# A neural codec's residual: diagonal products on sixteen 32x32 places of TensorE instead of four 64x64 places

## The chip, the core and the metric

One core of a Trainium2 chip runs the whole program. The time is device time in microseconds (us), the median of three runs; the profile is of one further execution. TensorE (PE in the profile, its weight loads PEld) multiplies into PSUM; VectorE (DVE), ScalarE (ACT) and GpSimd (POOL) do elementwise work; SyncE (SP) issues the transfers.

## What is computed

The reference, cut to what matters. B = 2 sequences of T = 16000 tokens with D = 512 channels; four codebooks of 8 rows each.

```python
def reference(x, dw_enc, codebooks, dw_dec):
    z = silu(depthwise_conv3(x, dw_enc))          # B, T, D
    res, q = z, zeros_like(z)
    for s in range(4):                            # four stages of a residual quantizer
        cb = codebooks[s]                         # 8, D
        d2 = sum(res*res) - 2*res @ cb.T + sum(cb*cb)
        sel = cb[d2.argmin(-1)]
        q, res = q + sel, res - sel
    return depthwise_conv3(q, dw_dec)             # bfloat16
```

All of it is bfloat16, so each `res - sel` is rounded to bfloat16, and the last choice depends on those roundings.

## The kernel before

**Tiles.** The 32000 tokens are cut into 18 tiles of G x 128 tokens, G = 8, 10, 12, then twelve of 16, then 12, 10, 8 (`SIZES`, L202). Channels lie on the partitions, in KT = 4 blocks of 128; each tile lives in slots of the large array `XR`/`XT`, 128 tokens to a group g, and z overwrites x there.

**Stages of a tile.** `load` (L625) brings x by transposing transfers on SP's queue. `front` and `front2` (L661, L694) make z: the three taps, two sums, exponential, reciprocal and gate, on ACT and DVE. `products` and `gram` (L722, L704) compute norms and scores of one group against the codebooks on TensorE, as 128x32 weights and 64 columns. `select` (L734) decides stages 0 to 2 from the scores of z and the codebooks' own products; it leaves one-hot choices in `OHALL`, and GpSimd lays them out anew in `OHDS` (L790, L802). `resid` (L889) makes the residual before the last stage, again on TensorE, and writes it over z; then `products` once more and the last choice (`decide3`), `windows` (L862: the transposed one-hots) and `back` (L977: two products per 128 tokens, a copy out of PSUM into `YB`, and a store).

**The residual** (`resid`). It runs over the four channel blocks; call one pass of `unit(i)` a unit. There are 18 x 4 = 72. The groups g of the tile are dealt to four row groups r = g mod 4, because the one-hots of group g stand on partitions 32r to 32r+31; each r has a PSUM bank of its own, with a tile's G/4 groups of 128 columns (512 columns at G = 16; 384 and 256 at G = 10; 256 at G = 8). Into each bank go, one after another:

- z times the identity (`IDENT`), z times 2^16 (`UP`), later z times -2^16 (`DOWN`): the diagonal products (L910 to L914). Adding and taking away the lifted z makes PSUM round as the reference does.
- four `picks` (L916 to L919): the chosen codebook rows, weights `WR[v]` with 32 rows x 128 channels, four row groups at once.

Before, a diagonal product takes 64 channels to 64 partitions. For even r the two halves stay where they are, for odd r they swap (`half[r % 2 ^ ...]`, L913); so two values of r and two halves make four products on four 64x64 places of the array. IDENT, UP and DOWN take 8 such products each per unit, 24 in all, each with its own weight load.

A unit is two steps: `first` (IDENT and UP for r = 0, 1, into the first pair of banks) and `second` (IDENT and UP for r = 2, 3, picks 0 to 2, DOWN for all, the last picks). Then ACT or DVE copies each pair of banks back into `XR` (L941). Since odd groups have their channels swapped in halves, everything that is multiplied with them has to be swapped alike: the copies of the codebook for the last scores (`CBM2` and the last 2 x 32 columns of `XR`, L434 to L444, read in `gram` at L717) and the weights `WR` (made by `SEL3` and `spread`, L505 to L528).

**Order.** `Plan` (L17) holds every step with its engine, an assumed cost and what it depends on. The order on each engine is not worked out at run time: `RANK` is a written-out list with one rank for each step, which sorts the five engines' queues (PE, ACT, DVE, POOL, SP), and `WHERE` has a letter for each of the 610 steps that may run on ACT or DVE (copies out of PSUM, taps, the +1). `order` walks the queues with the assumed costs, hands out PSUM banks and, where it foresees TensorE standing idle, puts in filling products (`fill`, L1060) that keep its clock up. Assumed costs of the residual are at L932 to L935.

Of the kernel before, what the change touches and what calls it, by code (L numbers as in the profile page):

```python
# [8 lines left out]
BF16 = mybir.dt.bfloat16  # L9
# [176 lines left out]
def kernel(  # L186
# [8 lines left out]
    nc = tc.nc  # L195
# [14 lines left out]
    HB = 32  # L210
    ZW = HB + NC
    ROWX = SLOTS * P + 2 * NC
# [10 lines left out]
    RANK = ("000002000403000a02020c030d010b01010k020c0a0d07060g0t0a070d0b0e050e03050Q0S0R0T0d170r1b0f0i0a0D0J0X0m0b01070j0p0v0E0G0V0c"  # L223
            "0h0w0C0H0L0M0U06050i090g0q0e0c0o0f0f0k08080b090l0m04030x070j0w0y0A0C0E0G0I0m0p0t090v06080k0n0N0O0P0B0K110l0o0G0W13140g0y"
            "0M0105060e0n0o0t0u0x0y0A0h0A0i0w000f0L080k040V0z0s0C241T0F0q0I090s2a0r2b0B270w200i0g0j040m0n0l0r0h0K0q0p0o0h0u0x0s0z0l0O"
            "0r0S0u0W0n0p131615181a1c1e100q1i0t1j1r1p1s1u1w1y1A120z0N0A1C1I1O1Q1S1U1W150C0S0D0F0U0W0G0H11100I0L13190N0R1a180V112Q2V31"
            "36381b1r1f1w1v1J1S1g1v1C1M1L0v0D0F0H0s0P0J0U0y1f0M0N0B0j0Q0T0R0X0B1h06070d030k050h0b0a09040i080214121710190z1b1d0E1m0F1t"
            "0H1v0I290u0x1E0v1G1V1J1X222326160E0V0J2d2f2g2i2j2l2n2p190O140Q2r2u2t2w2z2B2D1c0S170T0U1c1h0W101g1f13151k1l1c1d1p1u1k1m3B"
            "1o3F3H3K3O3Q1w1H1B1K1I1P1P1E1L1G1R1K2c5b260D1g1k111n1l1o1q0L210u0r0q0n0j0l0o0w0p0v0x0e0c0f0m0g0t0s1z1x0K1B1M1D1H1N0Q251L"
            "1K0J1F0O0P1P1R0R280T2c0X2I152H0K0M2s0P2v2y2A2C2F2G2J1a0X1e122N2P2M2O2R2T2U2W1d161j193033323537393o1f1e1t1h1i3u1x1j1l3z1A"  # L230
            "1q1r1C3I1s1t1D1E1u1x3U1z404c4e4o4r1S2022282a2e2c242d2z2x2p1X29262b2d141734181a3e3i3h3n3r3t3v1e1n1z1p3y3E3D3G3J3L3N3S1g1y"
            "1G1A3V3X414446484b1h1K1Q1L1M1T1V1N1O1U1X1R1T22211U1V2725272b4X25285557595e5n2l2o2u2s2y2w2u2B2y2E2A2w2K2G2R2K2z2x2v2O2J2D"
            "0z0J0G0M0H0E0A0y0L0K0N0D0C0P0O0F0B0I2m2h2o2e2E122q2L1i3x2x162k1b1d2K2S2X1m3C0Q1714120T0S0V1118100X130U0W1916150R3d3b3c3a"
            "3f1n3g3j1s3w1q3l1o3k3m3q3p3s1y3A1B3M1F3W1I471N4t1D1J4h1F1H4k4m4n4q4s4v454y1i1W24214D4G4I4K4M4O4Q4T1j292c2d4V535456585a5d"
            "1n2e5i2f2h2k2j2j2k2m2l2m2o2p2q2p2s2t2u2D2F632A2J676h6m6p6r302P312S352U3b342T322W2M37313r3e343a6J3e332T1P1Q4z20234S52505c"
            "5f5h4i5j1k2g2h2i5p5s5m5r5v5x5z5B1o2r5F2t5E5I5J5L5O5R5T1p2C2z2G2H2D2E2M2N2I2H2Q2T2N2M2W2X2R2Q36386F3b3c6P6R6T737c3n393M3u"
            "3Q3A3q3v3g3z3j3d3D3m3N3w3l3y3l443I3D1b1n1p1d1h1l1e1k1f1i1g1j1c1r1q1m1o1a3P3R423T4f1O494j1S514g4d4a434l4p4u4x265g1H1s1G1w"
            "1F1A1C1E1u1y1x1I1B1v1z1J1D1t1W4w4A4B4H234E4P2a5k4J4L4C4F4R4N4U4W2f5o2g5l2i5q2r612B682n2q5G2v2w5N5P5Q5S5W605w621q2I2C2L65"
            "6e6a6k6n6q6v6A1s332V396C6I6H6K6O6Q6S1t3d6X3g3i35363j3k373a3l3p3b3c3q3w3h3i3B3C7H3F3I7J7M7Q7U843V3z4d8C4a3M3G3X3D4b3K3x42"
            "3F433H3y4w424y453T2P2S6u2U2V6y6L6G6N6U6W701u3f323h747972777d7f7i7k1v3s3d3u7m7o7r7t7v7x7A1w3A3k3E3G3o3p3H3J3r3s3K3L3x3t3T"  # L240
            "3U3B3C41468n48498p8s8u8x8J4n3V4x434E48404t414B463W4z444L4h424S4i4T4k441V211U221M1X2a251T1R1O1Q24281W231N1l1m5u5y5D5t5M5A"
            "5H662F6E5K5V2n5C5U645X692L6M292e2j2k2h2o2f2m2b2q2r2i272l2n2g181r2s6b6d6g6c6l6i6j6o2O6V6s6w6t6f6x6z6B6D2X7h3071347b387l3f"
            "7I3m3o7j3t3x7w7z7y7C7E7L7O1x3O3v3S7T828186888a8c8g1y453G478i8k8l8o8q8t8w1C4c8A4e4g3N3O4i4j3Q3T4k4l3U3R4p4s403X4A4D9m4K4M"
            "9w9B9D9F9L4X9Q554r5b4v4i514n564q4m544p574s4j594t5t4F4r3P3R8b3W408d8m8r8v8y8B8D1z4f8G4h8F8H8K8M8O8R8T8V1A4m3S4o9194929698"
            "9b9e1B4C474F4G4b4a4H4I4d4c4O4P4g4f4V504m4o585daa5c5fadagaiakaq5o4C5s4G5v4K4x5y4I5E4M4F5w4H5B4N4L5F4O5J4R4D202J2H2L2x2F2G"
            "2E2N2K2C2t2v2I2y2O2B2A78757a767p7u7e7B3n877n7g7s7q7D7F7G7K3y8I2Q37322X2R352V382S2P2U3936333a312W307N7V7P3q7R807X853E8z89"
            "837S7W8e8f8h8j3J8E3L8L3P8W3W9p499u4q4r934u4v979d999f9h9l9n1D4J9s4N9q9t9v9A9C9E9H9K1E4U4j4W9N9P9T9Va0a2a41G5aa75e5g4y4x5h"
            "5ianao5j5k4Aar5l5m4D4B5q5raD5u5zaLaOaTb8bc5V52615569594U62566f5e506b5b6e5d4T6457665a4W4Q4R9I5253a1abacaeahajal1F5nav5pap"
            "auaxazaBaCaEaG1H5x4J5CaIaKaNaQaSaUaW1I5G4P5K5L4S4T5M5N4V4W5R5T4X505W5X53546568bG6a6cbRbWc5c7c96pce6s5n6D5t576C5v6G5y5a6x"
            "5q6E5u566r5m6w5r533j3z3v3o3f3w3i3h3c3m3u3g3s3p3e3n3r3k8N8S8Q8P8U8X90954eaf9c9i9a9g9j9k9o9r4la93R3N3B3O3S3P3A3J3C3M3Q3F3K"  # L250
            "3t3H3L3I3E9M9J9G9y9Ua39Oa54uas9S9R9z9x9X9Wa6a84wam4zaw4EaJ4LaX4Qb55A5DaV5H5Ib1b4b3b7b9bbbd1K5Qbf5Sbibkbhblbnbpbtbv1L63bx"
            "67bBbFbEbIbKbMbO1M6d5c6g6h5h5g6i6jc3c46k6lca5j6n6q5lck6u6vcq6z6AcCcEcMcPcR6Ud4725L735M597q627v665c7adA7i5U5b705J775O585O"
            "5Pbg5U60bubAbzbHbQbTbX1S6mc66oc8cccbcdcfcgchcj1U6t5o6ycmcpcrcsctcvcx226B5s6I6J5x5z6M6N5B5C6O6P5E5D6Q6W5H5I7576dw7c7ddDdJ"
            "dNdTdW1Q1V7tej7M6e7W6j5e7N6f7R6g5f7T6i7V6k5g7D697Fex5d484f3V3U4g4h3X46414c4a494d4745434e4bataAaFayb0aHaMb24Uc2b6aRaPbabm"
            "bebjbr58c14l4k4w4p4A4z4t4s4B4n4y4q4u4obobqbsbybwbJbDbS5fczbLbNbC51bUbVbPc05icB5kcl5pcy5wcI5AcW6F6HcH6K6LcJcLcKcOcQcScV1X"
            "6S5F6Vd0d2d3d5d7d9dbdc2171df74dgdjdidldodqdr2878dz7e7f5Q5R7g7h5S5T7k7m61607r7s64ef7w7Aew7E7JeKeNeOeReW1R2086fd8d6s8g6t5i"
            "8c6r8ffh5h8i6u8lfx5k8a6q8m6v5j6R6Td86Xdedmdndpdtdud6dv2479dx7bdydKdCdHdMdPdSdU257n5X7pe0e2e4e5e8ecee277ueh7x7yepes7C7GeA"
            "eC7H7K6d6c7Q7SeU6h838bff8hfjfkfofrft1P1W8ofv8v6y8z6A5m8q6w8rfy5l8A6B8C6C5n4P4K4R4v4I4X4N4S4M4Q4C4OcicocwcncUcucAcX5GdhcN"
            "cFcGcDcTdad1dd5KdB5NdF5PdL7j7ldV7oe3e7ebedegeidkek297z677Bemeneqereteveyez2a7IeB7LeGeHeFeIeLeQeT2b7UeX7X80f86l81856n6m87"
            "886pfe8j8kfufs8p8wfA8sfBfCfDfEfF1T238BfH8F6E8I6G5o8M6H8LfQ5q8N6I5p4E52554H51544V4J4G1J1OdEdGdIdsdRdXdOe165eoe65VdQ5W63ea"  # L260
            "e9el68eu6aeD6beE7O7PeJePeMeSeVf1f0f22c82f384f5f6f4f7f9fafbfc2d896o8efgfiflfmfnfpfq2e8nfw8t8u6xfz8x8yfG6z8D8E6DfI8G8HfJ6F"
            "8J8KfKfLfMfNfO1N268OfP8P6J8Q6K5r8R6L8S6M5s")
    WHERE = ("DADDDAAAADAAAADDDDDADDDDDDDDDDDAAAAAAAAAAAAAAADDDDADDDDDADDDDDDDDADAAAAAAAAAAAAAAAADADDDDDDDDADDDDDDADAADAAADADAADAAAAAA"
             "AAAAAAAAAAAAAAAAAAAAAAADDDDDADDADAADDDDDDDADADADDDDAADAAAAAAAAAAAAAAADAADAAAAAAAAAAAAAAAAAADDDDDADDDDDDDDADDDDADDDDDDDDA"
             "ADAAAAAAAAADAAAAAAAAAAAAAAAAAAAAAAAAAAADDDDDDDDDADDDDDDDDDDDDDDDDDDAADAAAAAAAADAAAAAAAADAAAAAAAAAAAAAAAAAAADDDDDDDDDDDDD"
             "DDDDADDDDDDDDDDDADAADDADAAAAAAAAAAADAAAAAAAAAADAAAAAAAADDDDDDDDDDDDDDDDDDDDDDDDDDDDDDAAADDDAADDAAAADAAADAAAAAAAAAADAAAAA"
             "AADDDDDDDDDDDDDDDDDDDDDDDDDADDDADDAAAAAAADDAAADADAADADDDDDAADADAAADAADDDDDDDDDDDDDDADDDAAAADDDDAAADADDDDDDDDADAADDDADADD"
             "AADDADAAAA")
# [42 lines left out]
    CBM2 = sb([P, 2 * KT, NC], BF16, "CBM2")  # L311
# [37 lines left out]
    HF = P // 2  # L349
    PICK = 1.25  # L350
    WR = [sb([P, D], BF16, f"WR{v}") for v in range(4)]
# [51 lines left out]

    def setup():
# [22 lines left out]
        for i in range(KT):  # L427
            bx = {}
            ptb = lambda bx=bx: ps(bx).bitcast(BF16)[:, 0:NC]
            j = add("PE", 0.2, key, lambda i=i, p=ptb: nc.tensor.transpose(p(), CB1[:, i * P:(i + 1) * P], IDENT[0:NC, 0:NC]),  # L430
                    ["CB1", "I"], [], take=("S", bx), mm=1)
            j2 = add("ACT", 0.25, key, lambda i=i, p=ptb: nc.scalar.copy(CBT[:, i, :], p()), [], [("CBT", i)], after=[j])
            add("ACT", 0.25, key, lambda i=i, p=ptb: nc.scalar.mul(CBM2[:, i, :], p(), -2.0), [], [("CBM2", i)], free=bx, after=[j2])
        for i in range(KT):  # L434
            bx = {}
            ptb = lambda bx=bx: ps(bx).bitcast(BF16)[:, 0:NC]

            def turned(i=i, p=ptb):
                for h in range(2):
# [660 lines left out]
```

## Time and profile before

| | |
|---|---|
| median of 3 runs (lowest, highest) | 584.66 us (579.47, 587.69) |
| the profiled execution | 584.51 us |
| its span, first to last instruction | 582.2 us |
| mean granted TensorE clock | 0.951 of full |
| TensorE products, and weight loads | 12463 each |
| of these diagonal products (L914) | 1728 |
| of these filling (L1062) | 224 |

A row of a group in the profile gives line, engine, operation, what is written and read with the shape, and the count; then the time in which at least one of them ran, the mean length of one in ns, and the engine's idle time just before them with what ended it. A product's length includes its way through the array, so several in a row overlap; what a step costs TensorE is read from start to start. `64*64 64x512` is a product with 64x64 weights and 64 rows of 512 columns. A row of waits gives who waited for whom, the total in us, how often, and the longest. A row of a stretch gives its bounds and length, then each engine's busy time with its count of instructions, the granted clock, the share of the transfer engines and GB/s.

### The profile page before, as it was taken

How to read it: one execution, taken by the hardware profiler on the slowest of the kernel's cores; microseconds unless marked ns; L12 is line 12 of the kernel's file. 1: busy time of each engine (PE TensorE's matmuls, PEld its weight loads, DVE VectorE, ACT ScalarE, POOL GpSimd, SP SyncE). 2: the span in 40 equal slices, each digit the busy share in tenths (PEclk: the TensorE clock that was granted, in tenths of full speed). 3: DMA queues.
4: the chain of work that ended last, by engine and by line, in shares of the span. 5: the costliest groups of instructions: out<-in, count | busy, mean ns of one | idle time of the engine just before them, and what ended most of it. 6: DMA issues, size and time to landing. Idle time of an engine off the chain costs nothing.

```text
span 582.2 us, 27464 instructions
## 1 busy us (share of the span) xinstructions
PE 473.8 (81%) x12463; PEld 226.6 (39%) x12463; DVE 538.6 (93%) x1021; ACT 534.2 (92%) x430; POOL 109.0 (19%) x140
## 2 busy tenths in 40 slices
PE   6475878878787798877987798888898798989995
PEld 4232334424434244333434253334343354444442
DVE  5999999999999899999999999998999899988552
ACT  3889999989999999999999999998999989988554
POOL 6232102202002303050303024211204102010000
PEclk9688779979999899899999999898999999999999
DMA  7444546544455466756667665857886640311455
GB/s 248 99 92 100 89 95 94 85 91 75 85 159 118 83 129 120 187 127 119 124 153 131 150 143 109 196 91 163 145 139 129 183 130 3 112 75 40 159 190 174
DMA packets 153384, 71.81 MB, mean 123 GB/s; under 512 B 144710, under 2 KB 144742, under 8 KB 153012
## 3 DMA queue, kind: packets, MB, share of 16 engines
q1 hardware_dynamic: 153052, 69.64, 54.4%
q8 instruction: 97, 1.59, 1.2%
q10 hardware_dynamic: 216, 0.43, 0.2%
q14 instruction: 19, 0.16, 0.1%
HBM read 2.79 MB, written 32.77 MB: 61 GB/s over the span
## 4 chain that ended last, share of the span: by engine, by line
DVE 28%; ACT 25%; SPq 17%; PE 17%; issue 8%; DMA 4%; POOL 0%; ACTq 0%; DVEq 0%; POOLq 0%
SPq L631 13%; DVE XR L402 8%; ACT EX L700 6%; ACT XR L941 6%; ACT EX L689 4%; ACT YB L1006 4%; PE banks L914 4%; PE banks L997 4%; DVE EX L402 3%; PE banks L719 3%; SPq L1034 3%; DVE EX L682 3%; DVE TA L682 3%; PE banks L919 3%; DMA XR<-in_x_dram 2%
## 5 line engine op out<-in xcount | busy, mean ns | idle before, releaser
L402 DVE TENSOR_TENSOR XR<-XR,EX 128x4096 bf16<-128x4096 bf16 (+3 forms) x72 | 145.8, 2029 | 0.9 <-ACT EX L700 0.5
L1006 ACT CAST YB<-banks 128x1024 bf16<-128x1024 f32 x117 | 116.3, 1055 | 10.7 <-PE banks L997 5.1
L802 POOL COPY OHDS<-OHALL 128x256 bf16<-128x256 bf16 (+3 forms) x36 | 63.8, 1774 | 318.1 <-DVE OHALL L402 314.8
L689 ACT ACTIVATE EX<-XR 128x4096 bf16<-128x4096 bf16 (+3 forms) x36 | 115.9, 3218 | 2.2 <-DVE XR L402 2.0
L941 ACT CAST XR<-banks 128x1024 bf16<-128x1024 f32 (+2 forms) x120 | 106.7, 952 | 10.5 <-PE banks L919 10.5
L700 ACT ACTIVATE EX<-EX 128x4096 bf16<-128x4096 bf16 (+3 forms) x36 | 115.5, 3214 | 0.5 <-DVE EX L691 0.3
L719 PE MATMUL banks<-XR 128*32 128x64 bf16 x8064 | 92.6, 199 | 14.1 <-DVE XR L402 7.1
L719 PEld LDWEIGHTS <-XR 128*32 128x32 bf16 x8064 | 77.6, 97 | 60.4 <-issue 47.6
L919 PE MATMUL banks<-OHR,WR 32*128 32x512 bf16 (+2 forms) x1152 | 81.9, 357 | 0.0
L402 DVE TENSOR_TENSOR EX<-TA,EX 128x4096 bf16<-128x4096 bf16 (+3 forms) x36 | 72.7, 2020 | 0.0
L914 PE MATMUL banks<-XR,IDENT 64*64 64x512 bf16 (+2 forms) x576 | 57.8, 377 | 17.0 <-ACT YB L1006 3.4
L997 PE MATMUL banks<-WDEC,OHW 128*128 128x512 bf16 x190 | 58.7, 393 | 15.0 <-ACT YB L1006 4.7
L1062 PE MATMUL banks<-MSK,IDENT 128*128 128x512 bf16 x224 | 66.2, 437 | 4.9 <-DVE MSK L413 3.8
L914 PE MATMUL banks<-XR,UP 64*64 64x512 bf16 (+2 forms) x576 | 55.4, 363 | 0.0
L682 DVE TENSOR_SCALAR TA<-XR,WENC 128x2048 bf16<-128x2048 bf16 (+3 forms) x67 | 45.5, 683 | 5.1 <-DMA XR<-in_x_dram 3.1
L919 PEld LDWEIGHTS <-WR 32*128 32x128 bf16 x1152 | 23.6, 92 | 58.8 <-issue 52.9
L682 DVE TENSOR_SCALAR EX<-XR,WENC 128x2048 bf16<-128x2048 bf16 (+3 forms) x62 | 41.6, 683 | 1.0 <-DMA out_dram<-YB 0.9
L682 DVE TENSOR_SCALAR XR<-XR,WENC 128x2048 bf16<-128x2048 bf16 (+3 forms) x62 | 41.9, 685 | 0.0
L914 PE MATMUL banks<-XR,DOWN 64*64 64x512 bf16 (+2 forms) x576 | 41.4, 363 | 0.0
L691 DVE TENSOR_SCALAR EX<-EX 128x4096 bf16<-128x4096 bf16 (+3 forms) x36 | 39.5, 1101 | 0.0
L914 PEld LDWEIGHTS <-IDENT 64*64 64x64 bf16 x576 | 21.2, 105 | 44.8 <-issue 37.1
L1062 PEld LDWEIGHTS <-IDENT 128*128 128x128 bf16 x224 | 22.3, 109 | 32.1 <-issue 16.3
(137 smaller groups left out, 600.0 us busy)
## 6 DMA issues: line engine op xcount, KB each, us to landing
out_dram<-YB SPq DMA_DIRECT2D x34, 448.0 KB
out_dram<-YB SPq DMA_DIRECT2D x28, 512.0 KB
XR<-in_x_dram SPq DMA_TRANSPOSE x263
out_dram<-YB SPq DMA_DIRECT2D x28, 60.0 KB
XR<-in_x_dram SPq DMA_DIRECT2D x1, 1280.0 KB
XR<-in_x_dram SPq DMA_DIRECT2D x1, 1024.0 KB
out_dram<-YB SPq DMA_DIRECT2D x30, 2.0 KB
out_dram<-YB SPq DMA_DIRECT2D x2, 224.0 KB
```

Source lines behind the costliest of these rows:

```text
L402: add("DVE", cost, key, lambda: nc.vector.tensor_tensor(out=out, in0=a, in1=b, op=op), reads, writes, **kw)
L631: nc.sync.dma_start_transpose(out=X[:, :, g + 1, :], in_=src[g])
L682: lambda dst=to, src=src, w=w: nc.vector.tensor_scalar(out=dst, in0=src, scalar1=w, scalar2=None, op0=ALU.mult),
L689: add("ACT", act(nb * R), ("exp", n, i0), lambda: nc.scalar.activation(v(ex), Z, ACT.Exp, scale=-1.0), zt, ext + ["ACTTAB"], hold="E")
L700: nc.scalar.add_instruction(mybir.InstActivation(name=nc.get_next_instruction_name(), engine=mybir.EngineType.Activation, func=ACT.Reciprocal,
L719: nc.tensor.matmul(o[HB * q:HB * (q + 1), u * ZW:(u + 1) * ZW].rearrange("p (s c) -> p s c", s=2), lhsT=blk, rhs=both, start=False, stop=( ...
L914: nc.tensor.matmul(at(r)[to], lhsT=dia[h, h], rhs=Z[h, i, r:G:RG, :], start=start, stop=False)
L919: nc.tensor.matmul(at(r), lhsT=WR[v][g, i * P:(i + 1) * P], rhs=W[g, v // 3, 0:rows_of[r], :], start=False, stop=stop)
L941: either({"ACT": act_psum(2 * k * P), "DVE": dve(2 * k * P)}, key(1), lambda dst=dst, src=src: nc.scalar.copy(dst, src()), lambda dst=dst, ...
L997: nc.tensor.matmul(o, lhsT=W[:, k, PADC:PADC + P], rhs=WDEC[u], start=True, stop=not wrap)
L1006: either({"ACT": act_psum(1024), "DVE": dve(1024)}, key, lambda dst=dst, box=box: nc.scalar.copy(dst, ps(box)), lambda dst=dst, box=box: n ...
L1062: nc.tensor.matmul(PS[j // 2][:, 512 * (j % 2):512 * (j % 2) + NMK * ZW], lhsT=IDENT, rhs=MSK.rearrange("p u w -> p (u w)"), start=True, s ...
```

## The change

- The diagonal products become 32x32 blocks. Channels are rotated by r: quarter q of the block goes to quarter (q + r) mod 4 of the partitions, in the bank of r. Four quarters and four r are sixteen places. IDENT, UP and DOWN take 16 products each per unit, 48 in all.
- `first` now holds IDENT for r = 0, 1 alone (8 products); `second` has IDENT for r = 2, 3, UP for all four, the picks, DOWN and the last picks (56). The columns of a product and the picks are as before.
- What is multiplied with the residual is rotated alike: four copies of the codebook at the end of `XR` rather than two, written there straight from PSUM (`CBM2` and a copy by ACT go); twelve small transposes for each channel block rather than two; `SEL3` with four parts rather than two, and `spread` with seven products rather than three.
- Assumed costs follow (`DIAG`), and `RANK` and `WHERE` are new lists. One step fewer (the removed copy) is in `RANK`. In `WHERE` 306 letters are ACT's and 304 DVE's, where 315 and 295 were; of the `back` copies 112 and 14, where 117 and 9 were.

```diff
-    ROWX = SLOTS * P + 2 * NC
+    ROWX = SLOTS * P + 4 * NC
...
-    HF = P // 2
     PICK = 1.25
+    DIAG = 1.25
...
+    def turn_of(q, r):
+        at = HB * ((q + r) % RG)
+        return slice(at, at + HB)
...
             def turned(i=i, p=ptb):
-                for h in range(2):
-                    nc.tensor.transpose(p()[HF * h:HF * h + HF], CB1[:, i * P + HF * (1 - h):i * P + HF * (2 - h)], IDENT[0:NC, 0:NC])
+                for r in range(1, RG):
+                    for q in range(RG):
+                        to = turn_of(q, r)
+                        nc.tensor.transpose(p()[to, (r - 1) * NC:r * NC], CB1[:, i * P + HB * q:i * P + HB * (q + 1)], IDENT[0:NC, 0:NC])
...
-        add("ACT", 0.35, ("setup", 0.9, 0), lambda: nc.scalar.copy(XR[:, :, SLOTS * P:].rearrange("p i (h c) -> p i h c", c=NC),
-            CBM2.rearrange("p (h i) c -> p i h c", i=KT)), [("CBM2", i) for i in range(2 * KT)], ["ZC"])
...
-                    cb = SLOTS * P + (last and g % 2) * NC
+                    cb = SLOTS * P + (last and g % RG) * NC
...
-            def diagonal(dia, rs, start=False):
-                for r in rs:
-                    for h in half:
-                        to = half[r % 2 ^ (h is half[1])]
-                        nc.tensor.matmul(at(r)[to], lhsT=dia[h, h], rhs=Z[h, i, r:G:RG, :], start=start, stop=False)
+            def diagonal(dia, rs=range(RG), start=False):
+                for q in range(RG):
+                    for r in rs:
+                        h = turn_of(q, 0)
+                        nc.tensor.matmul(at(r)[turn_of(q, r)], lhsT=dia[h, h], rhs=Z[h, i, r:G:RG, :], start=start, stop=False)
...
             def first():
                 diagonal(IDENT, (0, 1), start=True)
-                diagonal(UP, (0, 1))
-
-            def second():
+
+            def products_of():
                 diagonal(IDENT, (2, 3), start=True)
-                diagonal(UP, (2, 3))
+                diagonal(UP)
                 for v in range(3):
                     picks(v)
-                diagonal(DOWN, range(RG))
+                diagonal(DOWN)
                 picks(3, stop=True)
-            c0, c1 = (mm(rows_of[2 * b] * P) for b in range(2))
+            c0 = mm(rows_of[0] * P)
...
-            j = add("PE", 2 * c0 + 0.09, key(0), first, ..., mm=8)
-            j = add("PE", 3 * c1 + c0 + RG * PICK * c0 + 0.28, key(1), second, ..., mm=32)
+            j = add("PE", DIAG * 0.5 * c0 + 0.09, key(0), first, ..., mm=8)
+            j = add("PE", DIAG * 2.5 * c0 + RG * PICK * c0 + 0.28, key(1), products_of, ..., mm=56)
```

129 lines of the change are left out of this document (65 added, 64 removed).

## Prediction

> **What bounds the kernel now.** I read the page first (engines, then the chain that ended last), then the busy time by stage, then the waits, then TensorE's instructions in order of time.
>
> ```profile
> span 582.2 us, 27464 instructions
> PE 473.8 (81%) x12463; PEld 226.6 (39%) x12463; DVE 538.6 (93%) x1021; ACT 534.2 (92%) x430; POOL 109.0 (19%) x140
> DVE 28%; ACT 25%; SPq 17%; PE 17%; issue 8%; DMA 4%; POOL 0%; ACTq 0%; DVEq 0%; POOLq 0%
> ```
>
> VectorE and ScalarE are busy 93% and 92% of the span, and the chain runs through them three times as long as through TensorE (53% against 17%). An average hides stages, so the next table cuts the span where the work changes:
>
> ```profile
> 40.00:440.00 400.00, 326.79 (x8773) 154.45 (x8772) 393.29 (x690) 391.96 (x288) 75.35 (x50) 0.95 0.61 122
> 440.00:519.70 79.70, 67.93 (x1950) 32.31 (x1949) 74.33 (x168) 76.77 (x63) 12.83 (x21) 0.98 0.39 105
> 519.70:531.30 11.60, 11.56 (x326) 5.42 (x326) 11.50 (x23) 9.36 (x9) 1.48 (x2) 1.00 0.27 94
> 531.30:571.90 40.60, 39.78 (x1127) 19.81 (x1125) 24.62 (x78) 24.97 (x31) 1.09 (x4) 1.00 0.41 141
> ```
>
> Columns after the length: PE, weight loads, DVE, ACT, POOL busy. From 40 to 440 us DVE idles 6.7 us of 400 and ACT 8.0: these two set the pace and TensorE has room. From 519.7 to 571.9 it is the reverse: TensorE is busy 51.3 of 52.2 us, and after 531.3, when the last front is done, DVE and ACT work 25 of 40.6 us each. This tail is TensorE's. The stage 440 to 519.7 lies between: DVE idles 5.4, ACT 2.9.
>
> How much do the element engines wait for TensorE before the tail (40 to 519.7 us)? These are the largest such rows, and two further rows that matter below:
>
> ```profile
> ACT XR L941 <- PE banks L919: 2.5, 3, 1.4
> ACT YB L1006 <- PE banks L1001: 1.5, 1, 1.5
> DVE RC L770 <- PE banks L823: 1.3, 1, 1.3
> ACT OT L816 <- PE banks L811: 1.2, 2, 0.9
> ACT YB L1006 <- PE banks L997: 1.1, 2, 0.7
> DVE TA L682 <- DMA XR<-in_x_dram: 3.1, 2, 2.4
> PE banks L719 <- issue: 6.1, 9, 1.0
> ```
>
> The first five add up to 7.6 us over two engines, so 3.8 us of time at most.
>
> **The change part by part.** *The diagonal products.* Two units of 512 columns, one whose halves stand together and one split by other work:
>
> ```profile
> 291.04 0.41 PE L914 MATMUL banks<-XR,IDENT 64*64 64x512 bf16 x4
> 291.59 0.70 PE L719 MATMUL banks<-XR 128*32 128x64 bf16 x64
> 292.23 0.60 PE L1062 MATMUL banks<-MSK,IDENT 128*128 128x512 bf16 x2
> 294.20 0.41 PE L914 MATMUL banks<-XR,IDENT 64*64 64x512 bf16 x4 [1.37 <-DVE PR L957]
> 296.40 0.41 PE L914 MATMUL banks<-XR,IDENT 64*64 64x512 bf16 x4
> 296.64 0.39 PE L914 MATMUL banks<-XR,UP 64*64 64x512 bf16 x4
> 296.85 0.39 PE L914 MATMUL banks<-XR,IDENT 64*64 64x512 bf16 x4
> 297.07 0.39 PE L914 MATMUL banks<-XR,UP 64*64 64x512 bf16 x4
> 297.39 0.83 PE L919 MATMUL banks<-OHR,WR 32*128 32x512 bf16 x12
> 298.14 0.63 PE L914 MATMUL banks<-XR,DOWN 64*64 64x512 bf16 x8
> 298.70 0.40 PE L919 MATMUL banks<-OHR,WR 32*128 32x512 bf16 x4
> 299.03 0.39 PE L997 MATMUL banks<-WDEC,OHW 128*128 128x512 bf16 x1
> 239.94 0.14 PEld L914 LDWEIGHTS <-DOWN 64*64 64x64 bf16 x8 [0.42 <-issue]
> L914 PEld LDWEIGHTS <-IDENT 64*64 64x64 bf16 x576 | 21.2, 105 | 44.8 <-issue 37.1
> ```
>
> I count start to start. Four products together (one round) cost 0.21 us when the next has the same shape (296.64 to 296.85), 0.24 first after another shape, and 0.32 when another shape follows (297.07 to 297.39): 0.11 for the turn. Joined, the unit is 0.24 + 0.21 + 0.22 + 0.32 + 0.75 + 0.56 + 0.33 = 2.63; split, 0.55 + 2.20 = 2.75. After the change sixteen products share the array, so a round does twice the work. What a round costs then the trace doesn't show; its new part is the time to issue 16 pairs rather than 4. Eight weight loads took 0.14 with 0.105 for one: 5 ns apart. The 64 pairs at 291.59 took 0.64 to the next start: at most 10 ns a pair. I take 5 ns (same line, nearest), which delays the last of 16 by 0.06 more where a turn follows; bounds 0 and 10. Joined: IDENT 0.24, UP 0.32 + 0.06, picks 0.75, DOWN 0.38, last picks 0.33 = 2.08, saving 0.55. Split: the first part is eight products in one round, 0.34; the second 0.23 + 0.38 + 0.75 + 0.38 + 0.33 = 2.07; saving 0.34, since half-filled rounds save nothing. Mean 0.45 a unit; with 10 ns 0.33, with none 0.57.
>
> At 256 columns the issue weighs more:
>
> ```profile
> 564.38 0.28 PE L914 MATMUL banks<-XR,IDENT 64*64 64x256 bf16 x4
> 564.49 0.28 PE L914 MATMUL banks<-XR,UP 64*64 64x256 bf16 x4
> 564.71 0.51 PE L919 MATMUL banks<-OHR,WR 32*128 32x256 bf16 x12
> 565.14 0.41 PE L914 MATMUL banks<-XR,DOWN 64*64 64x256 bf16 x8
> 565.49 0.29 PE L919 MATMUL banks<-OHR,WR 32*128 32x256 bf16 x4
> ```
>
> A round is 0.11, with a turn 0.22. Two rounds each of IDENT and UP, joined, are 3 x 0.11 + 0.22 = 0.55 and become 0.11 + 0.22 + 0.06 = 0.39; DOWN goes from 0.35 to 0.28: saving 0.23. Between, by columns, 0.34 for the tile of 12 and 0.28 for that of 10. How many units lie where:
>
> ```profile
> 440.00:519.70 79.70, 22.02 (x296) 7.03 (x297) 0.98 0.39 105
> 519.70:571.90 52.20, 15.05 (x280) 5.65 (x279) 1.00 0.38 131
> ```
>
> These are the diagonal products alone (L914), 24 a unit: 12 units in each stage. The tail's are four each of the last three tiles: 4 x (0.34 + 0.28 + 0.23) = **-3.4 us**, nothing covering them. The 12 before save 12 x 0.45 = 5.4 us of TensorE, which count only as far as DVE and ACT wait: at most 3.8 us, and half of those waits are for products that the change leaves alone; I take **-2.0** (bounds 0 and -3.8).
>
> *More instructions.* Each unit issues 48 diagonal pairs instead of 24: 1728 more in 72 units, and 48 in the setup. They have to be fetched:
>
> ```profile
> q8 instruction: 97, 1.59, 1.2%
> q8 instruction: 2, 0.03, 3.6%
> 559.15 0.51 PE L719 MATMUL banks<-XR 128*32 128x64 bf16 x43
> 560.18 0.35 PE L719 MATMUL banks<-XR 128*32 128x64 bf16 x21 [0.52 <-issue]
> ```
>
> 97 packets for 12463 pairs: one for 128. The second row is the stretch 557.7 to 561.4 us, which holds two packets and, between them, TensorE idle for 0.52 us without a wait: packets at most 3.7 us apart, and not quite fast enough. The tail has 326 + 1127 = 1453 pairs now and 288 more after, 13.6 packets; at 3.7 us that is 50.3 us against 52.2 - 3.4 = 48.8 that the products would need. I add **+1.5**. Bounds: 0, and a stall of 6.1 / 9 = 0.68 us (the row of L719's issue waits) for every one of 13.6 packets, +9.2. In the earlier stages the same stalls fall on an engine with room.
>
> *The rest.* POOL's larger SEL3, the 40 more transposes and 8 more `spread` products lie in the first 40 us, where they replace filling; they are due before the first residual. One ScalarE copy (L443) is gone, and the first products waited 0.3 us for it: nothing to a few tenths. The four cyclic copies of the codebook in `gram` cost the same address arithmetic. No DMA is added; SP's queue keeps its 263 loads but in a new order, and DVE waited only 3.1 us for them. Of the steps that may run on either engine 315 were ScalarE's and 306 are; five of the nine that move are `back` copies, 1.22 us on DVE for 1.06 on ACT:
>
> ```profile
> L1007 DVE CAST YB<-banks 128x1024 bf16<-128x1024 f32 x9 | 10.9, 1215 | 1.3 <-ACT YB L1006 1.3
> ```
>
> That is DVE +6.1 for these and, with the smaller ones both ways, some +4 against -1 for ACT. Three of the five are of the last three tiles, where DVE idles; I take **+0.5** (0 to +1.5).
>
> Sum, against the profiled execution's 584.5 us (2.3 outside its span; the median shown, 584.7, is the same): 584.5 - 3.4 - 2.0 + 1.5 + 0.5 = **581.1 us**.
>
> *A rule against it.* In the tail's rounds two row halves already write one bank, to different partitions, and four go together at 0.21 us. The Trainium skill (TensorEngine Tiling (Array Packing), Restrictions and Gotchas) says that different row tiles cannot access the same PSUM bank at once; the change has four row groups on each bank. By the rule the rounds of before would already take turns and the sum would end near 611 (the last rival), by the rows at 581; the trace speaks against it for two halves, and no run here shows four.
>
> **The rivals.** *Hidden.* The end is set by the elementwise work and the last tile's own chain, and the freed TensorE time turns into idle time. For it: 93% and 92%; against it: the saturated tail. 584.5, give or take the moved copies.
>
> *The fetch takes the place of the stream* (slower). Mechanism: pairs come at 128 per packet, and TensorE now eats them faster than they arrive. It decides from a period of 52.2 / 13.6 = 3.84 us a packet in the tail on, 0.14 above the bound read off. At a stall of 0.68 for each packet the tail gains 9.2 - 3.4 = 5.8: with the copies 590.8, and beyond 596 if the earlier stages stall likewise.
>
> *The backlog counts in full.* If TensorE's queue from 440 us on sets the end, 5.4 + 3.4 go through without a give-back: 575.7; some 3 us more if the stage before joins in.
>
> *Sixteen places don't run together,* four row groups on a bank taking turns: a round of 16 is then 4 x 0.21 = 0.86 where two rounds are 0.43: +1.29 a unit at 512, half of that at 256. 12 x 1.29 + 12 x 0.9 = +26: 611. Against: the two halves above, and the picks, four row groups on four banks at the full 0.21-0.25 a round.
>
> **How the numbers follow.** Forecast 0.48, hidden 0.18, fetch 0.15, full backlog 0.15, no sixteen places 0.04. Below 572.8 (2% under 584.5, about what a measurement of this kernel can tell from no change) lie half of the backlog case (with its 3 us more) and a little of the forecast: 0.10. Above 596.2: the last rival and a third of the fetch: 0.09. Within: 0.81. The range 571 to 593 takes in the forecast's bounds (584.5 - 3.4 - 3.8 = 577.3, and 584.5 - 3.4 + 9.2 + 1.5 = 591.8), the fetch's usual price and most of the backlog.
>
> **What would show it.** Right: L914 with 32*32 blocks, x16 to a round, IDENT to UP 0.21-0.24 us apart at 512 columns; a joined unit near 2.1 us, one of 256 near 1.34; TensorE still busy all of the tail, which is some 2 us shorter; about 111 instruction packets. Wrong: rounds of 0.4 us or more (no sixteen places); many issue gaps inside L719 and L914 in the last 50 us (fetch); TensorE idle in the tail while the end stands (hidden); ACT and DVE without waits for L919 and an end at 575 (backlog).

## The result, and the profile after

The changed kernel takes 589.86 us (median of 16 runs, 587.63 to 595.41) where the kernel before, on the same chip, takes 585.08 (16 runs): the ratio is 1.0101, 95% interval 1.0077 to 1.0124. It is slower by 4.8 us, where 3.4 less had been forecast (584.5 to 581.1). The profiled execution took 589.57 us, 2.0 of them outside its span. A few executions are slower as a whole, at a lower clock; the ratios and medians leave them out.

From the page of the changed kernel, the span, the engines and the instruction queue:

```profile
span 587.6 us, 30824 instructions
PE 432.5 (74%) x14078; PEld 216.1 (37%) x14185; DVE 541.9 (92%) x1030; ACT 535.9 (91%) x420; POOL 94.0 (16%) x140
q8 instruction: 110, 1.80, 1.3%
```

The span is 5.4 us longer. By this row TensorE works 41 us less than before (473.8), but that is too much: the trace lacks 107 of its products (14078 against 14185 weight loads). Two runs further down, of the same kernel with 64 and 32 pairs more, have every record and show 455.2 and 451.0 us. The two engines that set the pace have more to do: DVE 3.3 us, ACT 1.7. The instruction packets went from 97 to 110.

Next, the stretches of the changed kernel, with the same bounds up to 519.7 us. Its last front ends at 535.4, not at 531.3. Then one row of the kernel before, for comparison: all between 40 us and its last front.

```profile
40.00:440.00 400.00, 291.70 (x9528) 142.94 (x9594) 389.07 (x684) 385.90 (x272) 66.10 (x68) 0.92 0.64 121
440.00:519.70 79.70, 66.39 (x2458) 34.08 (x2474) 78.68 (x177) 77.62 (x63) 10.55 (x20) 1.00 0.45 108
535.40:576.60 41.20, 35.84 (x1262) 18.12 (x1273) 23.49 (x70) 22.10 (x27) 1.14 (x5) 0.96 0.44 149
40.00:535.40 495.40, 371.13 (x12487) 183.96 (x12574) 481.84 (x890) 478.63 (x348) 77.30 (x90) 0.93 0.59 116
```

```profile
40.00:531.30 491.30, 406.28 (x11047) 192.17 (x11046) 479.11 (x879) 478.09 (x358) 89.66 (x73) 0.96 0.57 118
```

Up to the last front the changed kernel needs 4.1 us more (495.4 against 491.3). DVE's share of it is 2.7 us more work (481.84 against 479.11) and 1.4 us more idle time; ACT has 0.5 more work and 3.6 more idle time. In the tail TensorE's busy time fell from 39.78 us of 40.6 to 35.84 of 41.2, so the shorter stream is there. But of the 5.4 us left idle (0.8 before), 2.5 are places where a product is missing from the trace. From the last front to the end it is 52.2 us, not 50.9.

Did the rounds become what was forecast? TensorE's instructions of the changed kernel in order of time: a joined unit of 512 columns, a split one, and a split one of 256 with its first half.

```profile
459.94 0.43 PE L920 MATMUL banks<-XR,IDENT 32*32 32x512 bf16 x16
460.16 0.42 PE L920 MATMUL banks<-XR,UP 32*32 32x512 bf16 x16
460.52 0.82 PE L925 MATMUL banks<-OHR,WR 32*128 32x512 bf16 x12
461.27 0.43 PE L920 MATMUL banks<-XR,DOWN 32*32 32x512 bf16 x16
461.64 0.40 PE L925 MATMUL banks<-OHR,WR 32*128 32x512 bf16 x4
...
491.81 0.41 PE L920 MATMUL banks<-XR,IDENT 32*32 32x512 bf16 x8
491.84 0.59 PE L920 MATMUL banks<-XR,UP 32*32 32x512 bf16 x16
492.36 0.83 PE L925 MATMUL banks<-OHR,WR 32*128 32x512 bf16 x12
```

```profile
563.79 0.30 PE L920 MATMUL banks<-XR,IDENT 32*32 32x256 bf16 x8
564.02 0.82 PE L1002 MATMUL banks<-WDEC,XR 128*128 128x512 bf16 x2
564.77 0.30 PE L920 MATMUL banks<-XR,IDENT 32*32 32x256 bf16 x8
564.80 0.38 PE L920 MATMUL banks<-XR,UP 32*32 32x256 bf16 x16
565.12 0.51 PE L925 MATMUL banks<-OHR,WR 32*128 32x256 bf16 x12
565.55 0.33 PE L920 MATMUL banks<-XR,DOWN 32*32 32x256 bf16 x16
565.81 0.29 PE L925 MATMUL banks<-OHR,WR 32*128 32x256 bf16 x4
```

Sixteen products take 0.22 us to the next of the same shape (459.94 to 460.16), as four took before. DOWN with its turn is 0.37 at 512 columns (461.27 to 461.64) and 0.26 at 256; 0.38 and 0.28 had been forecast. So the array does hold sixteen products at once, the four row groups of one bank among them.

Where TensorE is late, by the waits over the whole span: first of the kernel before, then of the changed kernel, and of this its `back` copies on DVE.

```profile
ACT XR L941 <- PE banks L919: 10.5, 10, 2.8
PE banks L719 <- issue: 6.6, 10, 1.0
DVE RR L956 <- PE banks L719: 3.6, 4, 1.6
DVE E L754 <- PE banks L719: 0.9, 1, 0.9
```

```profile
ACT XR L946 <- PE banks L925: 13.0, 16, 2.2
DVE XR L947 <- PE banks L925: 10.2, 6, 5.3
PE banks L726 <- issue: 9.7, 15, 1.8
```

```profile
L1012 DVE CAST YB<-banks 128x1024 bf16<-128x1024 f32 x14 | 17.0, 1220 | 4.7 <-PE banks L1002 3.1 <-ACT XR L946 0.8 <-DMA out_dram<-YB 0.5
```

There are more waits for the residual, on ACT (L941 before, L946 after) and on DVE (L942 before, 6.5 us in all; L947 after). Of DVE's 10.2 us, 5.3 are one wait at 544.7 us, in the tail, where DVE has time to spare.

TensorE's gaps marked "issue" (it idles and waits for nothing that the profile shows) need care. Counting all over 50 ns, I find 8.3 us in 14 places before and 22.4 in 99 after. But in 77 of the 99 (9.9 us) a weight load lies between the two neighbours whose product is not in the trace: these are missing records, not stalls. That leaves 12.5 us in 22 places; in the last 60 us, 0.5 before and 2.0 after. All of these places, before and after, lie where 95 or 96 pairs are left over when the weight loads so far are counted in groups of 128: at the end of an instruction packet, as the fourth group of experiments shows. One in the tail, at full length:

```profile
538.77 0.28 PE L861 MATMUL banks<-IDENT,OHDS 128*128 128x128 bf16 x2 [0.55 <-DVE OHDS L401]
540.46 0.23 PE L861 MATMUL banks<-IDENT,OHDS 128*128 128x128 bf16 x1 [1.41 <-issue]
```

### The profile page after: what moved, and what is told of

Same layout as the page of the kernel before. It is cut to its first block, busy times and chain, and to the rows that moved or that the text cites. A ratio compares the mean times of both kernels' runs of the same rounds, so it can differ in the third digit from the quotient of the medians.

```text
span 587.6 us, 30824 instructions
## 1 busy us (share of the span) xinstructions
PE 432.5 (74%) x14078; PEld 216.1 (37%) x14185; DVE 541.9 (92%) x1030; ACT 535.9 (91%) x420; POOL 94.0 (16%) x140
## 5 line engine op out<-in xcount | busy, mean ns | idle before, releaser
L1011 ACT CAST YB<-banks 128x1024 bf16<-128x1024 f32 x112 | 110.9, 1035 | 14.2 <-PE banks L1002 5.6
L946 ACT CAST XR<-banks 128x1024 bf16<-128x1024 f32 (+2 forms) x121 | 108.3, 950 | 13.0 <-PE banks L925 13.0
L809 POOL COPY OHDS<-OHALL 128x256 bf16<-128x256 bf16 (+3 forms) x36 | 57.6, 1599 | 322.7 <-DVE OHALL L401 322.7
L925 PE MATMUL banks<-OHR,WR 32*128 32x512 bf16 (+2 forms) x1152 | 86.9, 372 | 0.9 <-issue 0.9
L920 PE MATMUL banks<-XR,IDENT 32*32 32x512 bf16 (+2 forms) x1152 | 52.2, 373 | 21.7 <-ACT XR L946 8.2
L1002 PE MATMUL banks<-WDEC,OHW 128*128 128x512 bf16 x145 | 48.3, 392 | 14.1 <-ACT YB L1011 4.2
L1067 PE MATMUL banks<-MSK,IDENT 128*128 128x512 bf16 x142 | 46.1, 439 | 5.6 <-POOL XR L391 3.0
L920 PE MATMUL banks<-XR,UP 32*32 32x512 bf16 (+2 forms) x1152 | 38.6, 371 | 0.0
L719 PE MATMUL banks<-MSK,IDENT 128*128 128x512 bf16 (+2 forms) x59 | 22.2, 376 | 18.6 <-ACT XR L946 7.0
L920 PEld LDWEIGHTS <-IDENT 32*32 32x32 bf16 x1152 | 17.3, 88 | 47.0 <-issue 42.0
L920 PE MATMUL banks<-XR,DOWN 32*32 32x512 bf16 (+2 forms) x1152 | 31.6, 375 | 0.5 <-issue 0.5
```

The lines of the kernel that those rows point to most:

```text
L809: add("POOL", 1.5, key(4.2), lambda s=s, two=two, b=b, GT=GT: nc.gpsimd.tensor_copy(OHD[b][:, 0, 0:GT, 2 * s:2 * s + 2, :], two), [("OHA", ...
L920: nc.tensor.matmul(at(r)[turn_of(q, r)], lhsT=dia[h, h], rhs=Z[h, i, r:G:RG, :], start=start, stop=False)
L925: nc.tensor.matmul(at(r), lhsT=WR[v][g, i * P:(i + 1) * P], rhs=W[g, v // 3, 0:rows_of[r], :], start=False, stop=stop)
L946: either({"ACT": act_psum(2 * k * P), "DVE": dve(2 * k * P)}, key(1), lambda dst=dst, src=src: nc.scalar.copy(dst, src()), lambda dst=dst, ...
L1002: nc.tensor.matmul(o, lhsT=W[:, k, PADC:PADC + P], rhs=WDEC[u], start=True, stop=not wrap)
L1011: either({"ACT": act_psum(1024), "DVE": dve(1024)}, key, lambda dst=dst, box=box: nc.scalar.copy(dst, ps(box)), lambda dst=dst, box=box: n ...
```

## The experiments

Each ratio is to the kernel before on the same chip, five rounds each, with its 95% interval. The medians of before were 583.6 to 584.4 us.

### First: lists, count of pairs, or clock

*The new layout with the lists of before,* and *the layout of before with the new lists.* The rank of the copy that one of them lacks is taken out or put in.

```diff
 # the changed kernel, RANK and WHERE as before, and ahead of key = ("setup", 0.95, 0):
+        del plan.ranks[len(plan.steps)]
```

> The sixteen-place products with the queues of before (its lists; the rank of the removed copy is taken out). Fetch theory (1728 more pairs starve TensorE of instructions and let its clock fall): the last front ends near 531 us as before, the issue gaps of TensorE grow from 8 us in all towards 20, the tail is no shorter than 51 us; 584 to 589 us. List theory (the new lists put more copies ahead of the last front, and that is the loss): the tail is 2 to 3 us shorter than before, 580 to 583 us.

> The 64x64 products of before with the queues of after (a rank for the extra copy right behind the codebook's copies). List theory: the last front is late by 4 us as in after, and TensorE's longer units come on top; 590 to 594 us. Fetch theory: without the extra pairs the stalls stay near 8 us and the tail near 51 us; 583 to 587 us.

Measured: 600.27 us, 1.0258 (1.0213 to 1.0302), and 594.13, 1.0158 (1.0118 to 1.0198). The first is above both of its forecasts; the second is at the edge of what was expected if the new lists themselves lose, and its last front does end late, at 536.0 us. Either list loses with the other layout; by the ratios the layout alone costs 15 us, and the new lists win back 9 of them.

*The kernel before with its products cut by columns* (UP in two, DOWN in three): 1632 more pairs, the same streamed columns, lists and rotation.

```diff
+                parts = 1 if start else 3 if dia is DOWN else 2
+                for c in range(parts):
                 for r in rs:
...
-                        nc.tensor.matmul(at(r)[to], lhsT=dia[h, h], rhs=Z[h, i, r:G:RG, :], start=start, stop=False)
+                        nc.tensor.matmul(at(r)[to, k0 * P:k1 * P], lhsT=dia[h, h], rhs=Z[h, i, r + RG * k0:min(G, r + RG * k1):RG, :], start=start, stop=False)
```

> The kernel before with each UP product cut into two along its columns and each DOWN product into three, so that 1632 pairs are added and nothing else changes: places, lists, copies and streamed columns stay. Fetch theory: issue gaps grow to 15 to 20 us, some of them in the tail, and the clock falls; 587 to 591 us. List theory: the instructions alone cost at most 1 us; 584 to 586.5 us.

Measured: 599.94 us, 1.0298 (1.0251 to 1.0346). The instruction queue and the waits of this kernel:

```profile
q8 instruction: 110, 1.80, 1.2%
```

```profile
PE banks L719 <- issue: 24.4, 30, 3.0
ACT XR L946 <- PE banks L924: 19.4, 19, 3.1
DVE E L754 <- PE banks L719: 9.7, 7, 2.5
DVE RR L961 <- PE banks L719: 8.4, 6, 2.8
```

With the packets of the changed kernel (110), the array used as before, it loses as much as the new layout on the old lists. The loss is not in the array: it is in how instructions arrive (TensorE's gaps at packet ends, missing records left out, are 32 us where before has 8.3), and the pace-setting engines feel it. DVE waits 9.7 and 8.4 us for the scores; before it waited 0.9 and 3.6.

*The changed kernel with more filling,* since the granted clock of its profile is 0.92 and that of before 0.951:

```diff
-    FILL, PACE, REST, AFTER = 0.22, 1.7, 0.6, 1.0
+    FILL, PACE, REST, AFTER = 0.22, 1.2, 0.2, 0.4
```

> The kernel after with the filling products put in sooner (274 more, the same lists). If the lower clock of its first 150 us and the dip at 541 us cost the time: granted clock up from 0.92 to 0.95, 585 to 587.5 us. Fetch theory without the clock: the filling products have to be fetched as well; 589 to 592 us.

Measured: 590.35 us, 1.0093 (1.0056 to 1.0129), at a clock of 0.963. The time is that of the changed kernel, so a higher clock alone gains nothing; the clock theory falls.

### Second: is it the rate, and where in the program

*Half of the scores left out* (two of four channel blocks, so the choices are made from half the channels): 4032 pairs fewer, so that instructions are plentiful. (TensorE has less to do as well; this experiment does not separate the two.) Once on the kernel before, once on the new layout with the old lists.

```diff
-            for i in range(KT):
+            for i in range(0, KT, 2):
                 for q in range(P // HB):
```

> The kernel before, with the products of the scores and norms taken over two of the four channel blocks only (the other two are left out): 4032 pairs fewer, the residual and the lists as they are. Fetch theory: the few issue gaps vanish and TensorE's tail shrinks; 574 to 580 us. Base for the next run.

> The sixteen-place products with the lists of before, and the same two channel blocks of the scores left out: about 10200 pairs. Fetch theory: with instructions no longer scarce the sixteen places show what they stream; 2 to 4 us under the run before it, where with all pairs the same layout was 17 us over. Rival (the 32x32 products cost time of themselves, in turns of the array, in weight loads or in banks): still 8 us or more over the run before it.

Measured: 579.47, 0.9917 (0.9886 to 0.9948), and 583.89, 0.9993 (0.9965 to 1.002). The gaps at packet ends are all but gone (0.2 and 0.6 us). What the layout costs on the old lists falls from 15 us to 4.4, between its two forecasts: most of it hangs on how the instructions come, but not all of it. What the rest is stays open.

*The cut products in tiles 0 to 14 alone (1392 more pairs), and in the last three tiles alone (240):*

```diff
-                parts = 1 if start else 3 if dia is DOWN else 2
+                parts = 1 if start or n >= 15 else 3 if dia is DOWN else 2
```

> The kernel before with UP and DOWN cut along their columns in the tiles 0 to 14 alone: 1392 pairs more, none in the last three tiles. If pairs hurt only where TensorE sets the pace (my step: the earlier stages have room): 584 to 586 us. If TensorE's gaps reach VectorE and ScalarE everywhere: 594 to 598 us, nearly all of the 16 us that the cut cost in all tiles.

> The same cut in the last three tiles alone: 240 pairs more. If pairs hurt only in the tail: 588 us or more, up to the whole 16 us. If they hurt everywhere alike, in proportion: 585 to 587.5 us.

Measured: 598.38, 1.0227 (1.018 to 1.0275), and 590.44, 1.0109 (1.007 to 1.0148). The early tiles lose 14 us, though TensorE's mean load leaves room there; the late ones 6.

### Third: filling, the changed kernel with plentiful instructions, a small addition

*More filling with half of the scores left out,* on the new layout with the old lists and on before (the edits above together):

> The sixteen-place products with the lists of before and two of the four channel blocks of the scores left out, as in the earlier run, and filling products put in sooner (285 more). There it was 583.9 us at a granted clock of 0.90, 4.4 us over the same cut of the kernel before (579.5 at 0.92). Clock theory (the shorter stream drops TensorE under the gate more often, above all from 90 to 150 us): clock 0.95 or more, 578 to 581 us. If the rest has another cause: 583 us or more.

> Control: the kernel before with the same two channel blocks of the scores left out and the same sooner filling (249 more). Clock theory: it was disturbed less, 577.5 to 580 us. If filling helps every kernel with few instructions alike, the distance to the run before this one stays at 4 us.

Measured: 583.58, 1.0001 (0.9976 to 1.0026), at a clock of 0.952; and 581.9, 0.9963 (0.9939 to 0.9986), at 0.972. The clock gains nothing here either: the first kernel's time stays, and before so cut gets 2.4 us slower, for a reason not looked into. The distance between the two shrinks from 4.4 us to 1.7.

*The changed kernel with half of the scores left out:*

> The kernel after with its own lists and the same two channel blocks of the scores left out: 4032 pairs fewer. Fetch theory: its lists were laid out for the shorter units, and without the scarcity they should gain what they were made for; 574 to 579 us, below the same cut of the kernel before (579.5). If the new lists lose by themselves (more copies ahead of the last front): 583 to 588 us.

Measured: 583.28, 0.9994 (0.997 to 1.0018). With instructions plentiful the new layout with its own lists does not show its gain; it is 3.8 us slower than before cut alike (579.47), or 4.5 by the two ratios. That is what had been expected if the new lists lose by themselves. The engines' row of before so cut, and of the changed kernel so cut:

```profile
PE 441.3 (76%) x8359; PEld 192.5 (33%) x8431; DVE 539.2 (93%) x1021; ACT 533.8 (92%) x430; POOL 106.4 (18%) x140
```

```profile
PE 420.9 (72%) x10069; PEld 182.6 (31%) x10153; DVE 542.5 (93%) x1030; ACT 536.3 (92%) x420; POOL 94.1 (16%) x140
```

TensorE has 20 us less to do (both traces lack some of its products, 72 and 84) and nothing comes of it; DVE has 3.3 more and ACT 2.5. No gap at a packet end is left in the changed kernel so cut. Its last front is late all the same. Here is when the last front ends in eight profiles, and DVE's work from 40 us up to it, all in us:

| lists | kernel | last front ends | DVE's work | DVE idle |
|---|---|---|---|---|
| old | before | 531.3 | 479.1 | 12.2 |
| old | before, 128 more pairs (fourth group) | 529.3 | 477.5 | 11.8 |
| old | before, half of the scores | 530.1 | 478.8 | 11.3 |
| old | new layout, half of the scores | 530.9 | 478.8 | 12.1 |
| new | layout of before | 536.0 | 483.9 | 12.1 |
| new | changed kernel | 535.4 | 481.8 | 13.6 |
| new | changed kernel, more filling | 536.9 | 483.2 | 13.7 |
| new | changed kernel, half of the scores | 536.2 | 483.7 | 12.5 |

With the new lists DVE has more to do ahead of the last front, whatever the layout and however plentiful the instructions. In all twenty profiles of this document DVE's work up to there is 477.5 to 480.4 us with the old lists and 481.8 to 483.9 with the new ones.

*Only UP cut in two* (576 more pairs):

```diff
-                parts = 1 if start else 3 if dia is DOWN else 2
+                parts = 2 if dia is UP else 1
```

> Dose: the kernel before with each UP product alone cut into two along its columns, 576 pairs more (8 a unit), nothing else changed. The cut with 1632 pairs more cost 16 us. In proportion: 589 to 591 us. If the kernel has slack in its instructions up to some count: 584 to 587 us. If it stands right at the edge already: 592 us or more.

Measured: 594.34, 1.0189 (1.0149 to 1.0229). 240 pairs cost 6 us, 576 cost 11, 1632 cost 16: whatever costs is not proportional to the pairs. That broke the theory of a plain backlog.

### Fourth: the number of pairs, or where the packets end

A packet holds 128 pairs (16 KB, by the trace), and the order counts them: `CHUNK, FIRST, FETCH = 128, 33, 4.2` (L25), and `late` (L107) puts off a step that reaches past the end of a packet. By these numbers packets end where 128 - 33 = 95 pairs are left over, and there TensorE's gaps lie in the traces. So the lists of before were found for packets that end at certain products. All of the additions above also moved these ends. To move them and nothing else, some of the first filling products, which lie in the first 50 to 70 us where TensorE has nothing better to do, are cut by columns: 32 or 64 of them in two, for 32 and 64 more pairs, 48 or 64 in three, for 96 and 128. No rank, no letter and no streamed column changes, and the order does not learn of the added pairs.

```diff
         for _ in range(k):
+            parts = 2 if filled[0] < 64 else 1
+            filled[0] += 1
+            for c in range(parts):
+                c0, c1 = (NMK * v // parts for v in (c, c + 1))
-            nc.tensor.matmul(PS[j // 2][:, 512 * (j % 2):512 * (j % 2) + NMK * ZW], lhsT=IDENT, rhs=MSK.rearrange("p u w -> p (u w)"),
+                nc.tensor.matmul(PS[j // 2][:, 512 * (j % 2) + c0 * ZW:512 * (j % 2) + c1 * ZW], lhsT=IDENT, rhs=MSK[:, c0:c1, :].rearrange("p u w -> p (u w)"),
                              start=True, stop=True)
```

> The kernel before with the first 32 filling products in two: boundaries moved by a quarter of a packet. Count of pairs: 584 to 586 us. Place of the boundaries: between before and the half-packet shift, 587 to 593 us.

> The kernel before, with each of the first 64 filling products (they lie in the first 53 us, where TensorE has nothing else to do) given as two products of 256 columns: 64 more pairs, the same streamed columns, the lists untouched, so that every boundary of the 128-pair instruction packets behind them lies half a packet earlier in the program. If the count of pairs is what costs (fetch backlog), 64 pairs in idle time cost nothing: 584 to 586 us. If the place of the packet boundaries in the program is what costs (the lists put waits there), nearly as much as the small additions cost so far: 590 to 595 us, with the issue gaps of TensorE growing from 8 to 20 us or more.

> The kernel before, with each of the first 64 filling products given as three products (192, 128 and 192 columns or so): 128 more pairs, one whole packet, so the boundaries fall where they fell. Count of pairs: nothing, or, if h1 costs, twice what it costs. Place of the boundaries: back at 584 to 586 us although it has more pairs than h1.

> The changed kernel with the same 64 pairs added among its first filling products. Count of pairs: as the changed kernel, 589 to 591 us. Place of the boundaries: its own lists were found for its own boundaries, so it too loses when these are moved: 595 us or more; if it doesn't, its lists never fitted its boundaries, and 588 to 592 us.

> The changed kernel with the first 32 filling products in two parts: 32 more pairs, the packet boundaries behind them a quarter of a packet earlier in the program. If the lists of the changed kernel fit its own boundaries as well as those of before fit theirs: 591 to 595 us (before lost 7.0 us by the same shift). If its boundaries lie badly as they are, so that this is the 5 us that it lost, a shift can as well gain: under 588 us here or in the run beside it.

> The changed kernel with the first 48 filling products in three parts: 96 more pairs, boundaries three quarters of a packet earlier, which is a quarter of a packet later in the program. Lists that fit: 591 to 596 us. Boundaries that lie badly as they are: under 588 us here or in the run beside it.

| more pairs in idle time | kernel before | changed kernel |
|---|---|---|
| 0 | 584.2 | 589.9, 1.0101 (1.0077 to 1.0124) |
| 32 | 591.28, 1.0121 (1.0077 to 1.0164) | 598.55, 1.0242 (1.0197 to 1.0287) |
| 64 | 593.01, 1.0148 (1.0116 to 1.018) | 595.28, 1.0177 (1.014 to 1.0213) |
| 96 | | 591.54, 1.012 (1.0074 to 1.0165) |
| 128 | 583.83, 0.9998 (0.9977 to 1.002) | |

64 pairs cost before 8.8 us, twice as many cost nothing. The number is not what costs; the place is. With 64 more pairs TensorE's gaps are 27.7 us in 28 places, all again with 95 pairs left over (8.3 us in 14 places before, 8.1 in 13 with 128 more). The same stretch of the program, first in the kernel before, then with 64 pairs more:

```profile
337.03 0.39 PE L712 MATMUL banks<-MSK,IDENT 128*128 128x512 bf16 x1
337.35 1.43 PE L719 MATMUL banks<-XR 128*32 128x64 bf16 x128
338.71 0.41 PE L914 MATMUL banks<-XR,IDENT 64*64 64x512 bf16 x4
338.95 0.39 PE L914 MATMUL banks<-XR,UP 64*64 64x512 bf16 x4
339.26 0.83 PE L919 MATMUL banks<-OHR,WR 32*128 32x512 bf16 x12
```

```profile
341.35 0.39 PE L712 MATMUL banks<-MSK,IDENT 128*128 128x512 bf16 x1
341.67 1.22 PE L719 MATMUL banks<-XR 128*32 128x64 bf16 x128
342.82 0.41 PE L914 MATMUL banks<-XR,IDENT 64*64 64x512 bf16 x4
343.06 0.39 PE L914 MATMUL banks<-XR,UP 64*64 64x512 bf16 x4
343.38 0.40 PE L919 MATMUL banks<-OHR,WR 32*128 32x512 bf16 x4
346.14 1.04 PE L919 MATMUL banks<-OHR,WR 32*128 32x512 bf16 x8 [2.37 <-issue]
```

The 128 scores are through in 1.2 to 1.4 us. Before, the packets end elsewhere and the twelve picks run on. With the ends moved, TensorE stands still after the fourth pick for 2.37 us; in the trace an instruction packet starts to move at 343.84, just after the stall begins, and TensorE goes on at 346.14, 1.4 us after it has landed. The waits of the two shifted kernels, half a packet and then a whole one:

```profile
PE banks L719 <- issue: 16.1, 19, 1.8
ACT XR L941 <- PE banks L919: 19.1, 19, 2.8
DVE E L754 <- PE banks L719: 7.4, 6, 3.8
```

```profile
PE banks L719 <- issue: 7.7, 10, 1.6
ACT XR L941 <- PE banks L919: 11.7, 13, 2.8
DVE E L754 <- PE banks L719: 0.9, 1, 0.9
```

The changed kernel gains at none of the three shifts, 1.0177 and 1.0242 against its 1.0101, and at 96 pairs 1.012, which the intervals don't tell from it. So its lists were fitted to its packets too, and its 5 us are not a bad place of the packets that one of these shifts gives back.

More filling on the changed kernel put 274 pairs in, all along, and lost nothing. There the order counts the added pairs and hands out banks and filling anew: its gaps at packet ends are 9.3 us, where the changed kernel has 12.5. That its time stays at 590.35 us with fewer gaps and a higher clock speaks against both as the main part of the loss.

## Why the prediction was wrong

**The stream: right.** The forecast for a joined unit of 512 columns was 2.08 us; the rows give 0.22 + 0.36 + 0.75 + 0.37 = 1.70 up to the last picks, with their 0.33 (taken from before) 2.03. A bank shared by four row groups costs nothing: a round is 0.22, where the rival at 611 had 0.86. The rule of the Trainium skill beside that rival (TensorEngine Tiling (Array Packing), Restrictions and Gotchas), by which different row tiles cannot access the same PSUM bank at once, is not borne out by these rounds.

**-3.4 in the tail, "nothing covering them": too much; +1.5 for the fetch: about right.** From start to start, idle time left out, the diagonal products of the last three tiles took 13.7 us before and take 11.2: 2.5 less. The sum took their units as joined. In the new order all four of the last tile are split: 0.23 + 0.03 + 0.32 + 0.26 = 0.84 us by the rows above, where a joined one took some 0.91 before, so less than 0.1 is saved and not 0.23. TensorE's gaps at packet ends grew by 1.5 us in the tail (0.5 to 2.0), as set down. That it fits is luck: they lie at single packets, 1.41 us of them at 540.46, and the sum was worked out from the mean period. What the sum left out is that TensorE, once faster, waits in the tail for ACT and DVE: 1.8 us where it waited 0.2. The two together more than eat up the 2.5, and the tail is 1.3 us longer instead of 1.9 shorter.

**-2.0 from the stage before the tail: did not come.** From 440 to 519.7 us the idle time of DVE and ACT did shrink, 5.4 to 1.0 and 2.9 to 2.1 us. But by then their work had been put off: the last front ends 4.1 us later. What an engine waits less in one stretch is no gain if the same engine arrives there with more left to do.

**"In the earlier stages the same stalls fall on an engine with room": wrong as a rule, but not what cost the 4.8 us.** TensorE's mean load from 40 to 440 us (327 of 400) says nothing of when its results are due. The cut products in tiles 0 to 14 cost 14 us; 64 pairs of no length cost 8.8, and the waits of ACT and DVE for TensorE rise with them (10.5 to 19.1, 0.9 to 7.4). A stall of 2 us in the midst of a unit is passed on to the copy and the decision behind it, and DVE and ACT, at 93% and 92%, have little to make it up with. In the changed kernel itself, whose lists fit its packets, TensorE's gaps at packet ends up to the last front grew only from 7.7 to 10.5 us; DVE waits there 3.8 us for TensorE and ACT 8.3, where they waited 2.8 and 9.6.

**+0.5 for the new lists: the step that failed.** The prediction had DVE at +4 and took 0.5, because three of the five moved `back` copies were put in the last three tiles, where DVE idles. In the trace three of the five lie ahead of the last front (8 copies there, 5 before), and other steps moved to DVE as well. DVE is the engine that sets the pace up to there, and it has 2.7 us more to do in this profile (481.84 against 479.11). Over the table's eight profiles the new lists give it 4.6 us more on average, and the last front ends 5.7 us later. So the 4.1 us by which the last front is late here, the larger part of the loss, come with the new lists, and 2.7 of them are DVE's work. Of its 1.4 us of added idle time, waits for loads and stores make up more than all (4.0 to 7.6 us); "no DMA is added" had put them at nothing. The other profiles with the new lists don't show that, so it may be this execution's own. Lists with the old division of work, fitted to the new packets, weren't run; whether they would gain stays open.

**The rival that came nearest** in time is the fetch taking the place of the stream (590.8 against 589.9), and the 110 packets are there as well. That is mostly luck. It was to decide in the tail by the mean period, with 9.2 us of stalls; the gaps there are 2.0 us, at single packets, and most of the loss lies ahead of the tail and has another cause. "Hidden" is nearer in mechanism: with instructions plentiful, 20 us less of TensorE's work brought no time at all, and it had allowed for the moved copies.

## What to carry to other kernels

Count a change of TensorE's products in pairs as well as in columns: more and smaller products are more instructions to fetch, and a stretch of short products uses up a packet faster than the next one comes. Where an order was written out for packets that end at certain products, any insertion moves these ends; before laying a loss at the door of an edit, shift the same kernel by a few idle pairs, by half a packet and by a whole one, and see how much of the time hangs on that alone. When an edit comes with new lists, run the new lists on the old kernel too, and compare the work of the engine that sets the pace up to a fixed event. Before calling a gap a stall, compare the count of products with that of weight loads: where a product is missing, the trace shows a gap that wasn't there. And an engine's mean idle time is no room for a stall, as long as two others, busy 92% of the time, wait for its single results.

## What was not expected of the hardware

- The place of the packets' ends is worth 7 to 9 us (1.2 to 1.5%) to the kernel before, with no other work changed; a whole packet more restores the time to within 0.2%.
- TensorE's instructions run out at one place only: with 95 or 96 pairs left over of each 128. In before and in the shifted kernels, whose traces are whole, all of these gaps but one (0.7 us) lie there, and TensorE goes on 1.1 to 1.7 us after a packet has landed.
- In these twenty traces two instruction packets never follow one another faster than some 3.2 us, start to start: 3.37 is the shortest in the trace of before, 3.31 in those of the changed kernel and of the cut products, 3.21 in that of the cut products in tiles 0 to 14. That is 25 ns a pair. A round of sixteen streams in 0.22 us, 14 ns a pair, so such rounds run at full rate only while what has been fetched lasts.
- When half of the places are still filled by another step, the free ones start at once: UP begins 0.03 us after the second half of IDENT (491.81 to 491.84), where a full round takes 0.22.
